# First batch reordered, softmax division moved behind the matrix product, two merged steps per later head pair

## The chip, the cores and the metric

The kernel runs on one core of a Trainium2 chip. Its time is device microseconds of one execution, and the figure of a version is the median of its runs. TensorE (PE) does matrix products and transposes, VectorE (DVE), ScalarE (ACT) and GpSimd (POOL) the elementwise work, and SyncE (SP) issues every DMA. Each engine works through its own list of instructions in order and waits on semaphores for the others.

## The reference

Four batches of 576 tokens with 8 heads of 64 go through three blocks, each fed by the one before:

```python
scores = (q @ k.T) / 8 + alibi          # only 0 <= i-j < 128, else -1e9
attn = exp(scores - max); attn /= (sum + 1e-9); x = attn @ v      # x: B, S, 512
h = gelu(x @ w_in)                      # 1024 wide, halves u and v
v_n = layernorm(v) * g_ln; v_s = w_sg @ v_n + b_sg                # over the tokens
x = x + (u * v_s) @ w_out
xk, xr = token mixes of x with the token before it
out = sigmoid(xr @ w_r) * (relu(xk @ w_k) ** 2 @ w_v)
```

## The kernel before, in words

The program doesn't write the engines' instructions in order. It records operations (`K.mm`, `K.act`, `K.ts`, `K.dma` and so on), each with its engines, an estimated duration and the tiles it touches, and `Rec.schedule` then lays them out on the five engines with a planner. A planned operation starts when its inputs are there by the planner's estimate, and among those ready the one with the lowest due time goes first; `PRI` shifts the due time of all operations of one tile name, `ENG` the choice between engines for operations that two or three engines can do. The result is a fixed order on each engine. On the chip each engine goes through its order and waits where an input is late. SP's order is such a result as well.

Attention works on head pairs: pair `c` is heads 2c and 2c+1, four pairs to a batch, sixteen in all. For a pair, `s_bank` computes scores of query blocks 0 and 1, then of 2 and 3 (tile `s`: two PSUM banks, one per head, with 64-row products running two at a time), and `s_last` those of the last 64 queries of both heads. Each of a pair's nine score tiles goes through `s_tile`: one DVE instruction adds the mask and takes the row maximum, ACT takes the exponential and the row sum. After the ninth, `s_last` takes the reciprocals of the nine sums (`rin`) and multiplies each of the nine tiles `p` by its column of them, on DVE, POOL or ACT. `t1_step`, `t2_step` and `t4_step` transpose the tiles on PE and copy them to SBUF (`pf`); in heads from 8 on the two key blocks of a tile are added first, so there are fewer transposes. `av_step` multiplies by v (tile `a`, 64-column products, two at a time) and copies the result into `x`. `slot(c)` writes the steps of pair c and of pair c-1 into each other: score step, transposes, score step, `av_step`, `s_last`. The score tiles have two PSUM banks (`psS`, tag `s`), which `av_step` uses too, the transposes two (`psT`) and the large products four (`psD`, tag `d`).

In the first batch nothing but attention and the decoding of weights is there to do. Weights come as 64-bit floats for the most part and are decoded by ACT and DVE (`job`; tiles `st`, `wdec`) and split into a high and a low part. So that the granted clock of PE stays high there, `filler` puts in products that nobody reads (tile `wps`). `v_first` begins one product of the second block early: for the first 128 tokens, with the x of head pair 0. Then, for batch b, the steps of the second block (`moe1(b)`) and of the attention of batch b+1 are merged; all products of the second block have the name `d`. The third block (`phase2`, tiles `d`, `rps`, `vps`) comes last.

The lines touched: `PRI`, `ENG` and `NWARM` (L29 to L73), `dma` (L539), `s_bank` and `s_last` (L681 to L715), `av_step` (L767), `slot` (L810), `v_first` and `v_tile` (L860 to L900), and the start of the program from L1072 to L1122.

Of the kernel before, what the change touches and what calls it, by code (L numbers as in the profile page):

```python
# [20 lines left out]
P = 128  # L21
NC = DM // P
HS = S // 2
MW = 320
# [12 lines left out]
    ("rl", "act/dve/pool"): 111000, ("rps", "pe"): 6800, ("s", "pe"): -37200, ("st1", "sp"): 29800, ("sum", "dve"): -135300, ("t", "pe"): -900,
    ("tf", "pe"): -36000, ("tri", "pool"): 3500, ("u", "dve"): -86200, ("v", "dve"): -129400, ("vhl", "act/dve/pool"): -45400, ("vhl", "dve"): -65700,
    ("vhl", "dve/pool"): 5100, ("vps", "pe"): 13200, ("vsg", "dve"): -9100, ("vsg", "dve/pool"): -3900, ("w_in_t", "act/dve/pool"): -1200,
    ("w_in_t", "dve/pool"): -25500, ("w_out_t", "act/dve/pool"): -3600, ("w_out_t", "dve/pool"): 13000, ("w_r_t", "act/dve/pool"): 31700,  # L40
# [6 lines left out]
}  # L47
ENG = {
    ("gg", "act/dve/pool", "act"): -36800, ("gg", "dve/pool", "dve"): -10300, ("k2h", "act/dve/pool", "act"): 63400,
    ("k2h", "act/dve/pool", "dve"): 200, ("k2h", "act/dve/pool", "pool"): 5800, ("k2l", "dve/pool", "dve"): -5500, ("k2l", "dve/pool", "pool"): 1100,  # L50
    ("mask", "dve/pool", "dve"): -13500, ("mask", "dve/pool", "pool"): -157800, ("mask4", "dve/pool", "dve"): 31200,
    ("mask4", "dve/pool", "pool"): -24500, ("mt", "dve/pool", "dve"): -7700, ("mt", "dve/pool", "pool"): 20200, ("p", "dve/pool", "dve"): -400,
    ("p", "dve/pool", "pool"): -14300, ("p", "dve/pool/act", "dve"): 13600, ("p", "dve/pool/act", "pool"): -19400, ("pf", "act/dve", "act"): -9900,
    ("pf", "act/dve", "dve"): 2900, ("pf", "pool/dve", "pool"): 31900, ("pf1", "act/dve", "act"): -143000, ("pf1", "act/dve", "dve"): 1800,
    ("pf4", "act/dve", "dve"): 17100, ("pf4", "pool/dve", "dve"): -54300, ("pf4", "pool/dve", "pool"): -27600, ("rl", "act/dve/pool", "act"): -149000,
    ("rl", "act/dve/pool", "dve"): 13300, ("v", "dve/pool", "dve"): -58600, ("v", "dve/pool", "pool"): 6000, ("vhl", "act/dve/pool", "act"): 10600,
    ("vhl", "act/dve/pool", "dve"): 63200, ("vhl", "act/dve/pool", "pool"): -48100, ("vhl", "dve/pool", "dve"): -52100,
    ("vhl", "dve/pool", "pool"): -500, ("vsg", "dve/pool", "dve"): -5400, ("vsg", "dve/pool", "pool"): 2200, ("w_in_t", "act/dve/pool", "act"): 2400,
    ("w_in_t", "act/dve/pool", "dve"): -21000, ("w_in_t", "dve/pool", "dve"): 18300, ("w_in_t", "dve/pool", "pool"): -98500,
    ("w_out_t", "act/dve/pool", "act"): 5100, ("w_out_t", "act/dve/pool", "dve"): 67600, ("w_out_t", "act/dve/pool", "pool"): -8800,  # L60
    ("w_out_t", "dve/pool", "dve"): -6500, ("w_out_t", "dve/pool", "pool"): -29500, ("w_r_t", "act/dve/pool", "act"): 1800,
    ("w_r_t", "act/dve/pool", "dve"): 2500, ("w_r_t", "act/dve/pool", "pool"): -33900, ("w_r_t", "dve/pool", "dve"): 36800,
    ("w_r_t", "dve/pool", "pool"): 17500, ("w_sg_t", "act/dve/pool", "act"): -19200, ("w_sg_t", "act/dve/pool", "dve"): -5300,
    ("w_sg_t", "act/dve/pool", "pool"): -800, ("w_sg_t", "dve/pool", "dve"): 23300, ("w_sg_t", "dve/pool", "pool"): -12000,
    ("w_v_t", "act/dve/pool", "act"): 54500, ("w_v_t", "act/dve/pool", "dve"): -11700, ("w_v_t", "act/dve/pool", "pool"): -4800,
    ("w_v_t", "dve/pool", "dve"): 18100, ("w_v_t", "dve/pool", "pool"): 10600, ("wk", "act/dve/pool", "act"): -28900,
    ("wk", "act/dve/pool", "dve"): 39900, ("wk", "act/dve/pool", "pool"): 3200, ("wk", "dve/pool", "pool"): 47700, ("x", "act/dve", "act"): 31200,
    ("x", "act/dve", "dve"): -9800, ("xg", "act/dve/pool", "act"): 8000, ("xg", "act/dve/pool", "dve"): -31100, ("xk", "act/dve/pool", "act"): -9400,
    ("xk", "act/dve/pool", "pool"): 25000, ("xk", "dve/pool", "dve"): -11200, ("xk", "dve/pool", "pool"): 5100, ("xr", "act/dve/pool", "act"): -7800,
    ("xr", "act/dve/pool", "dve"): -115500, ("xr", "act/dve/pool", "pool"): 4400, ("xr", "dve/pool", "dve"): -130300,  # L70
    ("xr", "dve/pool", "pool"): 129000,
}
# [1150 lines left out]
```

## Time and profile before

| | us |
|---|---|
| median of 3 runs (lowest, highest) | 606.44 (606.31, 608.42) |
| the profiled execution | 603.6 |
| its span, first to last instruction | 601.9 |
| PE busy in the span | 586.0 |
| DVE, ACT, POOL busy | 407.3, 307.7, 188.0 |

The profile is of one execution. Busy time is the time in which at least one instruction of the engine runs; a share over the whole span is a mean over stages with different limits, so the stages have to be looked at apart. The chain of waits goes back from the last instruction to what released it, step by step. In a timeline a row is a run of like instructions, its start, its length, and in brackets how long the engine stood idle before it and for what. An exact fp32 product shows as two records in the trace, so `s x8` is a score step of four products, and `a x24` an `av_step` of twelve.

### The profile page before, as it was taken

The numbers are of one execution on the slowest core, as the hardware profiler recorded it, in microseconds if no ns is written. First come the engines' busy times: TensorE is split into PE (matmuls) and PEld (weight loads), VectorE is DVE, ScalarE is ACT, GpSimd is POOL, SyncE is SP. The second block draws the span as 40 slices with busy tenths as digits, with TensorE's granted clock in tenths as the row PEclk, the third lists the DMA queues.
The fourth block names the chain that finished last, engine by engine and source line by source line (L and its number), as shares of the span: only waits on it lengthen the run. The fifth ranks groups of instructions, "written<-read, shape, count | busy, mean of one in ns | idle before, by whom it ended". The sixth has DMA issues, their size and how long they took to land.

```text
span 601.9 us, 9953 instructions
## 1 busy us (share of the span) xinstructions
PE 586.0 (97%) x3542; PEld 485.1 (81%) x3542; DVE 407.3 (68%) x1105; ACT 307.7 (51%) x809; POOL 188.0 (31%) x340
## 2 busy tenths in 40 slices
PE   6888999999999999999999999999999999999997
PEld 3555678998789987999889988888888888888885
DVE  4887899885898858887699988980780382243120
ACT  2997888445783446742265457650432451361130
POOL 4352556242641523423032511420450150021010
PEclk8998999999999999999999999999999999999999
DMA  8954433104220231000652265330001100000100
GB/s 223 347 128 118 133 80 97 46 18 140 63 62 2 62 113 50 3 22 1 212 182 71 71 209 182 111 105 36 35 4 67 37 0 36 35 1 0 53 19 35
DMA packets 23281, 48.28 MB, mean 80 GB/s; under 512 B 4416, under 2 KB 13120, under 8 KB 22720
## 3 DMA queue, kind: packets, MB, share of 16 engines
q1 hardware_dynamic: 23232, 47.65, 26.0%
q8 instruction: 28, 0.46, 0.3%
q14 instruction: 21, 0.17, 0.1%
HBM read 38.20 MB, written 9.45 MB: 79 GB/s over the span
## 4 chain that ended last, share of the span: by engine, by line
PE 91%; DMA 3%; DVE 2%; SPq 1%; ACT 1%; issue 1%; POOL 0%; DVEq 0%; POOLq 0%
PE d L431 54%; PE vps L431 17%; PE rps L431 8%; PE s L431 6%; PE a L431 4%; PE tf L439 2%; DMA st<-in_w_in_dram 1%; DMA wraw<-in_w_sgT_dram 1%; SPq L541 1%; DMA rawqk<-in_qk_dram 1%; PE t L439 1%; DVE p L723 0%; POOL w_sg_t L475 0%; PE wps L551 0%; DVE wdec L509 0%
## 5 line engine op out<-in xcount | busy, mean ns | idle before, releaser
L431 PE MATMUL d<-xk,wk 128*128 128x512 f32 (+1 forms) x480 | 103.4, 368 | 0.0
L431 PEld LDWEIGHTS d<-xk,wk 128*128 128x128 f32 x480 | 84.7, 188 | 16.2
L431 PE MATMUL vps<-w_v_t,k2h 128*128 128x512 f32 x288 | 94.8, 396 | 0.0
L453 ACT ACTIVATE p<-p,nmax 128x128 f32<-128x128 f32 (+1 forms) x144 | 67.7, 472 | 22.9 <-DVE nmax L723 21.3
L473 DVE TENSOR_TENSOR r<-vps,r 128x512 f32<-128x512 f32 x18 | 12.3, 690 | 98.3 <-PE vps L431 98.3
L529 POOL TENSOR_SCALAR mt<-xc,mus 128x512 f32<-128x512 f32 (+7 forms) x59 | 45.6, 786 | 63.3 <-DVE k2l L473 36.6
L431 PEld LDWEIGHTS vps<-w_v_t,k2h 128*128 128x128 f32 x288 | 54.1, 188 | 12.7
L431 PE MATMUL d<-w_sg_t,vhl 128*128 128x288 f32 x448 | 63.9, 298 | 0.0
L431 PEld LDWEIGHTS d<-w_sg_t,vhl 128*128 128x128 f32 x448 | 60.4, 188 | 2.4 <-issue 1.6
L431 PE MATMUL d<-w_in_t,xg 128*128 128x512 f32 (+1 forms) x240 | 61.1, 405 | 0.1
L723 DVE CUSTOM_DVE_ANT_0 p<-s,mask 128x256 f32<-128x256 f32 (+1 forms) x144 | 49.9, 378 | 15.9 <-PE s L431 15.7
L453 ACT ACTIVATE rl<-d 128x512 f32<-128x512 f32 (+1 forms) x40 | 22.0, 554 | 72.5 <-PE d L431 67.1
L431 PE MATMUL vps<-w_v_t,k2l 128*128 128x512 f32 x144 | 57.0, 396 | 0.0
L431 PE MATMUL d<-xg,w_in_t 128*128 128x288 f32 x384 | 55.5, 299 | 0.0
L431 PEld LDWEIGHTS d<-xg,w_in_t 128*128 128x128 f32 x384 | 51.8, 188 | 3.9 <-issue 3.2
L431 PE MATMUL d<-gg,w_out_t 128*128 128x288 f32 x384 | 54.7, 297 | 0.0
L431 PE MATMUL s<-rawqk 64*128 64x256 f32 (+2 forms) x320 | 47.2, 388 | 7.5 <-DVE nmax L723 3.9
L431 PEld LDWEIGHTS d<-w_in_t,xg 128*128 128x128 f32 (+1 forms) x240 | 42.0, 180 | 14.9 <-issue 2.5
L431 PEld LDWEIGHTS d<-gg,w_out_t 128*128 128x128 f32 x384 | 51.8, 188 | 2.0 <-issue 1.9
L492 POOL TENSOR_SCALAR_AFFINE_SELECT pf<-pf 128x512 f32<-128x512 f32 (+2 forms) x78 | 41.0, 537 | 34.3 <-ACT pf L461 28.7
L431 PE MATMUL rps<-w_r_t,xr 128*128 128x512 f32 x216 | 50.9, 390 | 0.0
L431 PEld LDWEIGHTS rps<-w_r_t,xr 128*128 128x128 f32 x216 | 40.3, 188 | 8.7 <-ACT r L453 0.2
(116 smaller groups left out, 938.7 us busy)
## 6 DMA issues: line engine op xcount, KB each, us to landing
rawqk<-in_qk_dram SPq DMA_DIRECT2D x32, 288.0 KB, 4.8
rawv<-in_v_dram SPq DMA_DIRECT2D x32, 160.0 KB, 2.3
xs<-x SPq DMA_DIRECT2D x4, 1154.0 KB, 5.5
out_dram<-r SPq DMA_DIRECT2D x18, 256.0 KB, 2.0
st<-in_w_in_dram SPq DMA_DIRECT2D x8, 512.0 KB, 8.6
wraw<-in_w_k_dram SPq DMA_DIRECT2D x8, 512.0 KB, 5.0
wraw<-in_w_v_dram SPq DMA_DIRECT2D x8, 512.0 KB, 3.5
wraw<-in_w_out_dram SPq DMA_DIRECT2D x8, 256.0 KB, 3.1
```

The source lines that it names most:

```text
L431: pe.matmul(real(o), real(l), real(r), start=st, stop=sp, **ex)
L439: pe.transpose(real(o), real(i), real(d))
L453: nc.scalar.activation(real(out), real(in_), func, scale=scale, **kw)
L473: alts.append(("dve", self._dve(out.n, False), lambda: nc.vector.tensor_tensor(real(out), real(a), real(b), op)))
L492: nc.gpsimd.affine_select(out=real(out), in_=real(in_), pattern=[[0, rows], [sgn, n]], compare_op=cmp, fill=0.0, base=0, channel_multiplie ...
L529: alts.append(("pool", 240 + out.n if ptr else 150 + 0.83 * out.n, lambda: nc.gpsimd.tensor_scalar(real(out), real(a), real(s1), real(s2), ...
L541: return self.r.op([("sp", nbytes / 330.0, lambda: nc.sync.dma_start(out=real(out), in_=real(in_)))], [in_, *reads], [out, *writes], nomin ...
L723: K.raw("dve", 70 + w / 0.96, lambda: nc.vector.tensor_tensor_reduce(out=real(pw), in0=real(s), in1=real(ma), scale=-0.125, scalar=3.0e38, ...
```

## The change

Five parts. One: SP's first three DMAs are fixed: the two halves of q and k of pair 0, then `rel`, the table of distances from which the masks are made; all others come behind. Two: for pairs 0 to 3 the tiles `p` of the first 512 queries are no longer multiplied by the reciprocals. `r_rows` spreads the reciprocals over rows by eight small products with the identity (tile `rt`), copies them to SBUF, and the copy of `a` into `x` becomes a multiplication by them on DVE. The tile of the last 64 queries is multiplied as before. Three: `v_first` begins three of the five tiles of the second block's v half for batch 0, with each of the head pairs 0, 1, 2 in turn; the filler goes on until the fifth of these tiles. Four: for pairs from 5 on `slot` has two steps that use 64-wide products in place of four: `av_s` (the product with v of pair c-1 together with the scores of blocks 0 and 1 of pair c) and `s_rest` (the last 64 queries and blocks 2 and 3). Five: all numbers of the planner's tables are new, and the tables tell the first batch (`.0`) and the second block of batch 0 (`.1`) from the rest.

```diff
 PRI = {
-    ("xr", "act/dve/pool"): -2300, ("xr", "dve/pool"): -17600, ("xs0", "sp"): -70700, ("xs1", "sp"): 26500, ("xs2", "sp"): 18000,
...
+    ("xs0.1", "sp"): 49179, ("xs1", "sp"): 2862, ("xs2", "sp"): 8293, ("xs3", "sp"): 14178,
...
-NWARM = 12
+NWARM = 8
+RROW = 4
+MERGE = 5
...
-        return self.r.op([("sp", nbytes / 330.0, lambda: nc.sync.dma_start(out=real(out), in_=real(in_)))],
-                         [in_, *reads], [out, *writes], nominal=nominal)
+        o = self.r.op([("sp", nbytes / 330.0, lambda: nc.sync.dma_start(out=real(out), in_=real(in_)))],
+                      [in_, *reads], [out, *writes], nominal=nominal)
+        if len(self.FIRST) < 3:
+            o.order |= set(self.FIRST[-1:])
+            self.FIRST.append(o)
+        else:
+            o.order.add(self.FIRST[-1])
+        return o
...
-        for n, i, col in [(2 * c + j, i, 4 * j + i) for j in range(2) for i in range(4)] + [(2 * c, 4, 8)]:
+        RS[c] = r
+        for n, i, col in [(2 * c + j, i, 4 * j + i) for j in range(2) for i in range(4) if c >= RROW] + [(2 * c, 4, 8)]:
             pj = PT[n, i]
             K.ts(pj, pj, r[:, col:col + 1], 1.0, ALU.mult, ALU.mult, "dpa")
+    def r_rows(c):
+        t = T("psT", [P, 4, P], F32, "t", "rt")
+        K.mm([(t[64 * j:64 * j + 64, i, :], RS[c][:, 4 * j + i:4 * j + i + 1].spread(64), ident, True, True, SG)
+              for i in range(4) for j in range(2)])
+        rt = T("tp", [P, 512], F32, "t", "rt")
+        K.copy(rt, t.flat())
+        return rt
...
+    def s_rest(c):
+        bank, last = last_items(c, "psT")
+        banks, it = s_items(c, (2, 3))
+        K.mm(last + it)
+        s_tiles(c, (2, 3), banks)
+        rawqk.pop(c)
+        tail_tile(c, bank)
+    def av_s(c):
+        a, a4b, it = av_items(c - 1, "psT")
+        banks, its = s_items(c, (0, 1))
+        AV.append(K.mm(it + its))
+        av_copy(c - 1, a, a4b)
+        s_tiles(c, (0, 1), banks)
...
-        K.copy(x_t[b][:, ch, 1:513], a.flat())
+        if c < RROW:
+            K.tt(x_t[b][:, ch, 1:513], a.flat(), rt, ALU.mult)
+        else:
+            K.copy(x_t[b][:, ch, 1:513], a.flat())
...
+        m = cur and has and c >= MERGE
...
+        if m:
+            trans()
+            add(2800, av_s, c)
+            add(1500, s_rest, c)
+            add(0, tail)
+            return steps
...
-        if n == 3:
-            K.filler_end(wps[:, 0:256], *warm[:2], AV[1])
-            wps = T("psD", [P, 512], F32, "d", "wps")
-            v_first(0, 1)
-            K.filler(wps[:, 0:256], *warm)
+        if n > 1:
+            v_first(range(n - 2, n - 1))
```

What it makes of the order is seen in three places. SP at the start of the program, before (`st` is w_in, `rawqk` q and k of a pair, `rawv` v of a head):

```order
L541 DMA rel<-in_rel_dram 128x320
L541 DMA rawv<-in_v_dram 128x320 x4
L541 DMA ident<-in_ident_dram 128x128
L541 DMA rawqk<-in_qk_dram 64x1152 x2
L541 DMA st_152<-in_w_in_dram 128x1024
L541 DMA rawqk<-in_qk_dram 64x1152 x4
L541 DMA st_152<-in_w_in_dram 128x1024 x3
```

And now:

```order
L581 DMA rawqk_109<-in_qk_dram 64x1152 x2
L581 DMA rel<-in_rel_dram 128x320
L581 DMA st_132<-in_w_in_dram 128x1024 x3
L581 DMA rawqk<-in_qk_dram 64x1152 x2
L581 DMA ident<-in_ident_dram 128x128
```

q and k of pair 0 went from behind six DMAs to the front; three pieces of w_in moved ahead of q and k of pair 1, and the identity and v behind those.

PE behind the first `av_step`, before (`wps` from L551 is filler, `t` transposes, `s` scores):

```order
L431 MATMUL s<-rawqk 64x192 x2
L551 LDWEIGHTS tri
L551 MATMUL wps<-tri 128x256
L431 MATMUL s<-rawqk 128x128 x2
L431 MATMUL s<-rawqk 128x256 x2
L551 LDWEIGHTS tri
L551 MATMUL wps<-tri 128x256
```

The same place now, up to the products of the reciprocals (`rt`) ahead of the second `av_step`:

```order
L469 MATMUL s<-rawqk 64x192 x2
L477 MATMUL t<-ident,p 128x128 x7
L469 MATMUL s<-rawqk 128x128 x2
L469 MATMUL s<-rawqk 128x256 x2
L477 MATMUL t<-ident,p 128x128 x7
L469 MATMUL d<-w_in_t,xg 128x512 x6
L477 MATMUL tf_465<-ident,p 128x128
L469 MATMUL s<-rawqk 128x256 x4
L469 MATMUL d<-w_in_t,xg 128x512 x3
L469 MATMUL rt<-ident,rin 64x128 x8
```

Where filler stood, products `d` of the second block stand now; nine of them are placed ahead of the second `av_step`, 27 ahead of the end of the fourth, where there were none and nine. In all 86 filler and warm-up products have become 41.

PE from the `av_step` of pair 4 on, before (`a_1089` is its last part):

```order
L431 MATMUL a_1089<-pf_1006,rawv 64x64 x4
L431 MATMUL s<-rawqk 64x192 x2
L431 MATMUL d<-w_in_t,xg 128x512 x6
L431 MATMUL s<-rawqk 128x128 x2
L431 MATMUL s<-rawqk 128x256 x2
L431 MATMUL d<-w_in_t,xg 128x512 x6
L431 MATMUL d<-w_in_t,xg 64x512 x6
L439 MATMUL tf<-ident,p 128x128 x4
L431 MATMUL d<-w_in_t,xg 64x512 x6
L439 MATMUL tf<-ident,p 128x128 x4
L431 MATMUL s<-rawqk 128x256 x4
```

And now:

```order
L469 MATMUL a_978<-pf_940,rawv 64x64 x4
L469 MATMUL s<-rawqk 128x128 x2
L469 MATMUL s<-rawqk 128x256 x2
L469 MATMUL d<-w_in_t,xg 128x512 x12
L469 MATMUL s<-rawqk 64x192 x2
L469 MATMUL s<-rawqk 128x256 x4
L469 MATMUL d<-w_in_t,xg 64x512 x12
```

Three stretches of 64-wide products per pair have become two, and both score banks of pair 5, which stood ahead of the `av_step` of pair 4 before (those shown before are pair 6's), stand in and behind it now.

## Rows read from the trace of the kernel before

**Rows 1.** The page: busy time by engine, and the chain that ended last
```profile
PE 586.0 (97%) x3542; PEld 485.1 (81%) x3542; DVE 407.3 (68%) x1105; ACT 307.7 (51%) x809; POOL 188.0 (31%) x340
...
PE 91%; DMA 3%; DVE 2%; SPq 1%; ACT 1%; issue 1%; POOL 0%; DVEq 0%; POOLq 0%
```
**Rows 2.** Stretches: length, busy PE, PEld, DVE, ACT, POOL (instructions); clock, DMA share, GB/s
```profile
0.00:10.70 10.70, 6.73 (x20) 3.08 (x21) 3.25 (x10) 1.28 (x1) 6.02 (x17) 0.92 0.80 218
...
17.80:65.00 47.20, 40.17 (x311) 26.86 (x308) 40.19 (x146) 41.73 (x132) 19.16 (x31) 0.96 0.64 177
75.00:90.00 15.00, 15.00 (x103) 11.18 (x103) 14.66 (x48) 12.59 (x39) 8.30 (x18) 1.00 0.32 80
75.20:134.30 59.10, 59.10 (x453) 51.17 (x455) 53.46 (x168) 39.00 (x124) 27.47 (x53) 1.00 0.23 61
```
**Rows 3.** PE's waits over the whole span: us in total, times, longest
```profile
PE s L431 <- DVE nmax L723: 3.9, 4, 1.4
PE s L431 <- DMA rawqk<-in_qk_dram: 2.7, 1, 2.7
```
**Rows 4.** Groups of PE's instructions between 17.8 and 64.5 us: the filler
```profile
L551 PE MATMUL wps<-tri 128*128 128x256 bf16 x59 | 7.9, 273 | 0.0
```
**Rows 5.** Timeline of the start: start us, length us, what [idle before it]
```profile
3.58 1.19 SPq L541 DMA_DIRECT2D rawqk<-in_qk_dram  x2
...
8.96 2.39 PE L431 MATMUL s<-rawqk 64*128 64x128 f32 x8 [2.66 <-DMA rawqk<-in_qk_dram]
```
**Rows 6.** Timeline of ACT: the ninth exponential of pair 0 and of pair 4
```profile
17.37 0.46 ACT L453 ACTIVATE p<-p,nmax 128x192 f32<-128x192 f32 x1 [0.37 <-DVE nmax L723]
...
64.53 0.46 ACT L453 ACTIVATE p<-p,nmax 128x192 f32<-128x192 f32 x1 [0.28 <-DVE nmax L723]
```
**Rows 7.** Groups of ACT's instructions between 17.8 and 64.5 us
```profile
L536 ACT ACTIVATE p<-p,rin 128x256 f32<-128x256 f32 (+1 forms) x19 | 7.8, 474 | 0.8 <-DVE rin L713 0.8
...
L461 ACT COPY pf<-t 128x384 f32<-128x384 f32 (+1 forms) x11 | 5.4, 513 | 2.0 <-PE t L439 1.9
L625 ACT ACTIVATE wdec<-st 128x512 f32<-128x512 f32 x7 | 4.7, 668 | 0.0
L461 ACT COPY x<-a 128x512 f32<-128x512 f32 (+1 forms) x7 | 2.6, 415 | 0.0
```
**Rows 8.** Groups of DVE's instructions: the page's costliest, then three between 17.8 and 64.5
```profile
L473 DVE TENSOR_TENSOR r<-vps,r 128x512 f32<-128x512 f32 x18 | 12.3, 690 | 98.3 <-PE vps L431 98.3
...
L463 DVE COPY pf<-t 128x512 f32<-128x512 f32 (+1 forms) x5 | 3.2, 662 | 1.7 <-PE t L439 1.6
...
L473 DVE TENSOR_TENSOR p<-p 128x128 f32<-128x128 f32 (+1 forms) x10 | 2.9, 292 | 0.0
...
L526 DVE TENSOR_SCALAR p<-p,rin 128x256 f32<-128x256 f32 (+1 forms) x4 | 1.2, 329 | 0.0
```
**Rows 9.** Timeline of POOL and PE ahead of the av_step of pair 4
```profile
70.39 0.43 POOL L465 TENSOR_SCALAR w_out_t<-wdec 128x256 fp32r<-128x256 f32 x1
...
74.75 0.30 POOL L492 TENSOR_SCALAR_AFFINE_SELECT pf<-pf 128x128 f32<-128x128 f32 x1
...
75.13 1.08 PE L431 MATMUL a<-pf,rawv 128*64 128x256 f32 x8
```
**Rows 10.** Timeline of PE around the 64-wide steps of a later pair
```profile
110.83 3.88 PE L431 MATMUL d<-w_sg_t,vhl 128*128 128x288 f32 x28
...
116.54 0.54 PE L431 MATMUL s<-rawqk 64*64 64x192 f32 x4
117.02 1.32 PE L431 MATMUL d<-w_sg_t,vhl 128*128 128x288 f32 x8
118.27 0.93 PE L431 MATMUL s<-rawqk 64*128 64x128 f32 x8
119.12 1.85 PE L431 MATMUL d<-w_sg_t,vhl 128*128 128x288 f32 x12
...
121.78 1.13 PE L431 MATMUL s<-rawqk 64*128 64x256 f32 x8
```

More of the change, by code (lines that the diff above doesn't have):

```diff
@@ L37 @@
[L37 to L40, printed above, removed]
@@ L51 @@
[L51 to L54, printed above, removed]
@@ L137, in real @@
                 a = a.bitcast(x)
+            elif k == "bro":
+                a = a.to_broadcast([a.shape[0], x])
             elif x == 3:
@@ L192, in op @@
         o.port = {a[0]: self.ports(a[0], reads, writes, single) for a in alts}
-        o.lab = writes[0].base.name if writes and isinstance(writes[0], Vw) else "out"
+        o.lab = (writes[0].base.name if writes and isinstance(writes[0], Vw) else "out") + self.phase
         o.w0 = writes[0].base if writes and isinstance(writes[0], Vw) else None
@@ L690, in s_bank, with last_items, s_tiles @@
                 it.append((banks[j][:, k, :w], rawqk[c][r, 0, q0:q0 + P], rawqk[c][r, 1, k0:k0 + w], True, True, {}))
-        K.mm(it)
+        return banks, it
+    def last_items(c, pool):
+        bank = T(pool, [P, 2, 256], F32, "s" if pool == "psS" else "t", "s")
+        raw = rawqk[c]
+        it = []
+        for j in range(2):
+            r = slice(64 * j, 64 * j + 64)
+            it.append((bank[r, 0, 0:192], raw[r, 0, 512:576], raw[r, 1, 384:576], True, True, SG))
+        return bank, it
+    def s_tiles(c, ii, banks):
         if ii[0] == 0:
@@ L698, in s_bank, with tail_tile @@
                 s_tile(c, 2 * c + j, i, banks[j][:, k, :w], mask[:, h, c0:c0 + w], 4 * j + i)
[L700 to L708 removed]
+    def tail_tile(c, bank):
         s_tile(c, 2 * c, 4, bank[:, 0, 0:192], mask4[:, 2 * c % H // 2, :], 8)
@@ L779, in av_step, with av_copy @@
             a4.append((64 * j, rv, (p4[:, 1, j, :], p4[:, 0, j, :])))
-        a4b = T("psS", [P, 2, 256], F32, "s", "a4")[:, 0, 0:64]
-        AV.append(K.mm([x for y in zip(*its) for x in y] +
-                       [(a4b[r0:r0 + 64], rv[:, 3 + k, :], pf[k], k == 0, k == 1, SG) for k in range(2) for r0, rv, pf in a4]))
+        a4b = T(pool, [P, 2, 256], F32, "s" if pool == "psS" else "t", "a4")[:, 0, 0:64]
+        return a, a4b, ([x for y in zip(*its) for x in y] +
+                        [(a4b[r0:r0 + 64], rv[:, 3 + k, :], pf[k], k == 0, k == 1, SG) for k in range(2) for r0, rv, pf in a4])
+    def av_step(c):
+        a, a4b, it = av_items(c, "psS")
+        rt = r_rows(c) if c < RROW else None
+        AV.append(K.mm(it))
+        av_copy(c, a, a4b, rt)
+    def av_copy(c, a, a4b, rt=None):
+        b, ch = 2 * c // H, c % (H // 2)
         if ch == 0:
@@ L817, in add, with trans @@
             steps.append((w, lambda: f(*a)))
-        if cur:
-            add(1000, s_bank, c, (0, 1))
-        if has:
+        m = cur and has and c >= MERGE
+        def trans():
             for j in range(2):
@@ L824, in slot, with tail @@
             add(120, t4_step, prev)
+        def tail():
+            load_pair(c + 2)
+            load_v(2 * c + 2)
+            load_v(2 * c + 3)
+        if m:
[4 more added lines that the diff above has]
+            return steps
+        if cur:
+            add(1000, s_bank, c, (0, 1))
+        if has:
+            trans()
         if cur:
@@ L856, in v_mms, with v_first @@
         group(ps, [(XG[b][:, kk, pa, s * P:s * P + m], w_in_t[:, kk, pb, DM:DF]) for kk in ks for pa, pb in PASS], 6, ks[0] == 0, ks[-1] == NC - 1)
-    V0 = []
-    def v_first(a, z):
-        if not V0:
-            V0.append(T("psD", [P, 512], F32, "d"))
-        v_mms(V0[0], 0, 0, P, range(a, z))
-        return V0[0]
+    V0 = {}
+    def v_first(ks):
+        for s in range(3):
+            if s not in V0:
+                V0[s] = T("psD", [P, 512], F32, "d")
+            v_mms(V0[s], 0, s, P, ks)
     def moe1(b):
@@ L878, in v_tile @@
             m = min(P, S - s * P)
-            if b == 0 and s == 0:
-                ps = v_first(1, NC)
+            if b == 0 and s in V0:
+                ps = V0[s]
+                v_mms(ps, b, s, P, range(NC - 1, NC))
             else:
@@ L1122, in attn_gmlp_rwkv_kernel @@
     K.filler_end(wps[:, 0:256], *warm[:2], AV[3])
+    wps2 = T("psD", [P, 512], F32, "d", "wps")
+    K.filler(wps2[:, 0:256], *warm)
     for b in range(B):
@@ L1128, in attn_gmlp_rwkv_kernel, with v_last @@
         d = moe1(b)
+        R.phase = ".1" if b == 0 else ""
         if b == 0:
+            def v_last(f):
+                f()
+                K.filler_end(wps2[:, 0:256], *warm[:2], next(o for o in reversed(R.ops) if o.pe))
+            d[4] = (d[4][0], lambda f=d[4][1]: v_last(f))
             for i in range(5):
```

114 lines of the change are left out of this document (70 added, 44 removed), and 26 rows, old and new, of the table PRI.

## The prediction

> **What bounds the kernel now.** First the page: PE is busy 586.0 of 601.9 us, and 91% of the chain that ended last is PE [rows 1]. A change can gain where PE stands idle or does what nobody needs, or by taking work off PE. The view of PE's waits says where the idle time is: scores that wait for DVE to empty their banks, 3.9 us, and the first scores, which wait 2.7 us for q and k [rows 3], all ahead of 70 us; from 75.2 to 134.3 PE is busy for 59.1 of 59.1 us [rows 2]. So from there on every microsecond of PE work costs one, and before that PE isn't the bound. Third the stretches. I mark the first batch by ACT's ninth exponential of a pair: pair 0's ends at 17.8, pair 4's at 65.0 [rows 6]. In these 47.2 us ACT is busy 41.73 (88%), DVE 40.19 (85%), PE 40.17 of which 7.9 are filler [rows 2, 4]. PE does useful work for some 32 us there and fifteen are hollow. Fourth, behind 75 us DVE is close behind PE: 14.66 of 15 us from 75 to 90, 53.46 of 59.1 from 75.2 to 134.3 [rows 2].
>
> The sum below is made against the profiled execution (603.6 us, span 601.9); the median of the runs, 606.44, lies 2.8 above it, and I carry the difference over unchanged. I follow the moment at which the product with v of pair 4 begins, 75.2 in the trace of before [rows 9], since from there to the end PE has no gap in either version if the forecast holds.
>
> **1. q and k first.** Their DMAs are issued at 3.58 and the scores begin at 8.96 [rows 5]; now they are issued first. But that doesn't move pair 0's ninth exponential by as much: ACT's order puts three decodes of w_in ahead of it, and the third needs the third piece of w_in. Ahead of and with that piece SP issues 576 KB of q and k, 160 KB of distances and 3 x 512 KB of w_in, 2.33 MB. At 218 GB/s, the mean of the first 10.7 us [rows 2], that is there at 10.7. Then one decode of 0.67 [rows 7], three exponentials of about 0.5 and one of 0.46 [rows 6] with its sum read: 13.5, and 0.8 for waits on DVE between them: 14.3, against 17.8. Gain 3.5. Ends: 5.8, if the pieces land sooner and only ACT's own work counts, and 0, if the identity and q and k of pair 1, which are issued later than before, hold the transposes up.
>
> A rule of the Trainium skill speaks against it (DMA: Bandwidth & Descriptors, Queues, rings and completion order): a DMA is split over the rings of up to 16 engines, and completion isn't first-in first-out, so the first issued need not be the first complete. The trace has q and k land 5.4 us after their issue with six DMAs ahead of them, which fits a queue in order as well. By the rule, with nothing gained from the place in the queue, term 1 is 0; that is rival C.
>
> **2. The division behind the product.** Per pair eight multiplications of p go; one stays. Of 36 in the four pairs ACT has 19, together 7.8 us [rows 7], DVE 4, 1.2 us [rows 8], POOL the rest. By the order ACT keeps one: -7.4. Also off ACT go four 512-wide copies of `a` (all seven copies take 2.6 [rows 7], the four about 2.3); onto it come three copies of `rt` and four transposed tiles that DVE copied before, seven at 0.51 [rows 7], +3.6. ACT: 41.7 - 6.1 = 35.6. DVE loses 1.2, four of its five tile copies (2.6) and six of ten additions of p (1.8), and gains four multiplications of a PSUM tile (0.69 each by the nearest form, 2.8) and one copy of `rt` (0.7) [rows 8]: 40.2 - 2.1 = 38.1. I take the weight pieces that change engines as even. So DVE, not ACT, sets the least time of this stretch: 39.0 at the 97.7% it reaches from 75 to 90, 44.8 at the 85% that it has here. PE's share rises too: eight `rt` products are 16 records in pairs, 8 x 0.105 (128 columns at half of the 0.21 below) and a change of mode, 1.1 us, four times: 4.4; 18 products `d` are moved in (part 3), 4.3; its 32 become 41 by busy time. Busy time counts each pipelined end, and 4% of the stretch is at the lower clock [rows 2], so some 37 of real work. Three engines over 80% that wait for each other don't reach 97.7%. I take 43.0, a little under DVE's 85%: -4.2. Ends: -8.2, and 0 if in-order waits and not loads set the pace. What hides the 4.4 us of `rt` is the hollow; if that is gone, they count in full.
>
> The wait that this adds: the multiplication into `x` waits for `rt`, so for the ninth tile's sum. Behind it in DVE's order stand the high-low split of x and the score tiles of the next pair; the 0.5 us copy is planned ahead of `a`, which ends 2 us later, so I cost it at nothing.
>
> **3. Three v tiles early.** Between pair 4's ninth exponential and its product with v lie 10.2 us now (65.0 to 75.2), ended by a triangle cut on POOL at 74.75 [rows 9]. PE spends them on products `d`, two thirds of which are done before that now. So the chain through POOL is what is late next. Ahead of the cuts POOL has six other things from 70.39 on (first row of [rows 9]; lengths 0.43, 0.74, 0.46, 0.19, 0.59, 0.28, in all 2.7); in the new order scales and cuts follow each other directly there. 10.2 - 2.7 = 7.5. Gain 2.7; ends 0 (the chain unchanged) and 4.3 (the 18 products). The pair-4 product begins at 14.3 + 43.0 + 7.5 = 64.8, 10.4 earlier than 75.2.
>
> The count of `d` ahead of it is 36 in both orders, but pair 5's two score steps, 0.85 and 1.06 long by their starts, now come behind it: +1.9.
>
> **4. Merged steps.** A run of 28 `d` takes 3.82 to the next row's start, 0.136 each [rows 10]. From 117.02 to 119.12 there are 8 of them, 1.09, and a score step. Steps of 768 and 1024 columns last 0.85 and 1.06, so 256 columns take 0.21 and 768 take 0.63: 0.37 is lost, and a little in the first `d` behind, 0.4 for entering and leaving the 64-wide form. Per pair one such stretch goes. But inside the merged ones the form changes as well: the last-queries step takes 0.48 for 2 x 192 columns, 0.32, so 0.15 for a change inside; there are two per pair where there was one. 0.4 - 0.15 = 0.25, eleven pairs (5 to 15): -2.8. Ends: 0 and -4.4.
>
> The Trainium skill has the rule that any change of the tiling mode, not only of the tile, drains the array (TensorEngine Tiling (Array Packing), Key Properties). The trace agrees for the change inside a stretch (0.15). Taken as one price for each change, 0.2, a pair has 7 changes before and 6 now, and the term is -2.2, the result 0.6 later.
>
> **5. DVE behind 75 us.** From the product of pair 4 to that of pair 7 PE has 59.1 us now; 36 products of 0.136 fewer stand there and three merges: 53.4. DVE's work there I leave at 53.46, at its best share of 97.7%: 54.7. So PE waits 1.3. Ends 0, and 5.7 at the 90.5% that it has now.
>
> Fewer filler products (86 to 41) cost nothing while useful products stand in their place.
>
> **Sum:** -10.4 + 1.9 - 2.8 + 1.3 = -10.0. Profiled 593.6, median 596.4.
>
> **The rivals.**
> A: DVE runs as full in the first batch as behind it, 39.0 in place of 43.0: 592.4. For it: POOL has far less to do there. Against: nothing in the stretch is over 88% now.
> B: the stretch doesn't shrink, since each pair waits in turn for its scores, transposes and banks: +4.2, 600.6. For it: PE's waits for DVE to empty the score banks [rows 3], and the same banks now. Against: the nine scales stood in that chain, and are gone from it.
> C: the place in the queue gives nothing (above): +3.5, 599.9. By the same trace the first DMA's data was not the last to come.
> D: DVE holds PE behind 75 us with the share it has now: +4.4, 600.8. With B: 605.0, no change.
> E, the other side: the merged steps stall. In each of eleven `av_s` the scores of pair c stand behind the product with v of pair c-1, which needs the last cut on POOL; in the trace that cut ends at 75.05 and the product begins at 75.13 [rows 9], so nothing is to spare there. If PE waits 1.5 us at each, and the next softmax starts late by as much, 16.5 come back: 612.9. It decides from 0.9 us per pair. Against: PE has no wait behind 75 us, and there is other work for 7 us between the steps to put ahead.
> Also on that side, small: with filler gone the granted clock may fall to 1.2 GHz; 0.96 in the stretch now means 4 us of it [rows 2].
>
> **Chances.** Forecast (594 to 599) 0.50; A 0.18; B 0.11; C 0.06; D 0.06; B with D or the clock, no change, 0.04; E 0.05. About 0.5% or 3 us is what can be told from no change. Faster: 0.50 + 0.18 + 0.11 + 0.06 + 0.06 = 0.91, less 0.02 for the edges of B to D: 0.89. Same 0.06, slower 0.05. The range reaches from A with the early ends of 1 and 4 (589) to B with half of D (602.8, say 603). The forecast's own is 592 to 600.
>
> **What would show it.** In the new profile: first scores near 5 us and pair 0's ninth exponential near 14.3 (term 1); pair 4's near 57, ACT's L574 scales down to four or so ahead of that, DVE over 85% (term 2); the product with v of pair 4 near 65, with the cut on POOL ending just ahead (term 3); score stretches twice per pair (term 4); PE's waits between 65 and 115 about 1.3 us and DVE near 97% there (term 5). PE waits in `a` or `s` behind 120 us would make the prediction wrong, and so would pair 4's exponential later than 60 us.

## The result and the profile after

The changed kernel takes 601.65 us (median of 4 runs, 600.97 to 602.57), the kernel before 606.38 beside it: a ratio of 0.9916, 95% interval 0.9889 to 0.9943, or 4.7 us faster. That is the side that was forecast and about half of its size (10.0). The profiled execution took 602.57, its span is 600.8.

The page after: busy time, DMA's busy tenths in 40 slices of 15 us, and the chain.

```profile
PE 581.8 (97%) x3561; PEld 484.2 (81%) x3561; DVE 413.0 (69%) x1105; ACT 307.7 (51%) x800; POOL 184.4 (31%) x321
...
DMA  8974523222122130000652155150002000000100
...
PE 87%; DMA 6%; DVE 2%; POOL 1%; ACT 1%; SPq 1%; issue 0%; DVEq 0%; ACTq 0%
```

PE is 4.2 us less busy than in [rows 1] (filler and warm-up 6.1 less, `rt` 4.4 more, the rest in the clock and in overlaps), and DMA's share of the chain has doubled from 3% to 6%. PE's waits over the span (us in total, times, longest), against [rows 3]:

```profile
PE t L477 <- ACT pf L499: 2.9, 1, 2.9
PE a L469 <- POOL pf L530: 2.3, 3, 1.4
PE s L469 <- DMA rawqk<-in_qk_dram: 2.0, 3, 1.1
...
PE s L469 <- DVE nmax L813: 1.2, 1, 1.2
...
PE rps L469 <- ACT r L491: 1.2, 1, 1.2
...
PE a L469 <- POOL mv L1009: 0.7, 1, 0.7
...
PE d L469 <- DVE v L547: 0.5, 1, 0.5
```

The score banks are waited for 1.2 us in place of 3.9. New are 2.9 us for one copy of transposed tiles, and waits behind 75 us, where there were none. The stages, by the marks of the prediction (columns as in [rows 2]): the first batch from pair 0's ninth exponential to pair 4's, then to pair 4's product with v, to pair 5's, and to pair 7's.

```profile
14.97:62.51 47.54, 41.09 (x333) 28.71 (x333) 36.77 (x131) 34.89 (x115) 11.26 (x24) 0.93 0.74 188
62.51:67.78 5.27, 4.29 (x27) 3.27 (x26) 4.52 (x14) 4.23 (x12) 2.86 (x7) 1.00 0.93 229
67.78:86.15 18.37, 16.96 (x114) 12.56 (x114) 17.02 (x56) 13.04 (x39) 14.69 (x28) 1.00 0.29 80
86.15:124.39 38.24, 38.05 (x303) 33.98 (x303) 33.95 (x109) 26.99 (x88) 21.52 (x37) 1.00 0.27 76
```

ACT and DVE had as much work taken off as was reckoned (34.9 and 36.8 us busy, 35.6 and 38.1 forecast), and yet the stretch lasts 47.5 us, where it lasted 47.2 [rows 2]. So the load of neither sets it. What does is in the timelines (start, length, what, idle before it). First a row of SP in the kernel before, then SP, ACT, DVE, POOL and PE in the changed one:

```profile
18.12 1.06 SPq L541 DMA_DIRECT2D wraw<-in_w_sgT_dram  x2
```

```profile
18.19 0.47 SPq L581 DMA_DIRECT2D rawqk<-in_qk_dram  x1
24.35 0.80 SPq L581 DMA_DIRECT2D rawv<-in_v_dram  x2
25.20 1.75 SPq L581 DMA_DIRECT2D rawqk<-in_qk_dram  x3
27.16 4.44 SPq L581 DMA_DIRECT2D wraw<-in_w_sgT_dram  x2
...
37.99 0.43 ACT L499 CAST w_sg_t<-wraw 128x288 fp32r<-128x288 f32 x1 [2.92 <-DMA wraw<-in_w_sgT_dram]
...
38.46 0.78 DVE L511 TENSOR_TENSOR w_sg_t<-wraw,w_sg_t 128x288 fp32r<-128x288 f32 x1 [2.34 <-ACT w_sg_t L499]
...
37.61 0.43 POOL L503 TENSOR_SCALAR w_sg_t<-wraw 128x288 fp32r<-128x288 f32 x1 [6.04 <-DMA wraw<-in_w_sgT_dram]
...
39.63 1.11 PE L477 MATMUL t<-ident,p 128*128 128x128 f32 x4 [2.91 <-ACT pf L499]
```

Three engines stand still together for the first pieces of `w_sg`. In the new order SP issues these behind two loads of v; their buffers come free with pair 0's product, so SP stands from 18.7 to 24.35 and `w_sg` is issued at 27.16; its first piece is taken up at 37.6, 10 us later. It used to be issued at 18.12, ahead of the loads of v. Behind ACT's waiting instruction stand the copies of transposed tiles, and PE waits for those; from 39.7 to 43 the granted clock is then 0.5, that is 1.2 GHz.

### The profile page after: what moved, and what is told of

It reads as the page before. It is cut to its first block, busy times and chain, and to the rows that moved or that the text cites. A ratio compares the mean times of both kernels' runs of the same rounds, so it can differ in the third digit from the quotient of the medians.

```text
span 600.8 us, 9962 instructions
## 1 busy us (share of the span) xinstructions
PE 581.8 (97%) x3561; PEld 484.2 (81%) x3561; DVE 413.0 (69%) x1105; ACT 307.7 (51%) x800; POOL 184.4 (31%) x321
## 4 chain that ended last, share of the span: by engine, by line
PE 87%; DMA 6%; DVE 2%; POOL 1%; ACT 1%; SPq 1%; issue 0%; DVEq 0%; ACTq 0%
PE d L469 50%; PE vps L469 17%; PE rps L469 8%; PE s L469 5%; PE a L469 5%; DMA st<-in_w_in_dram 2%; DMA rawqk<-in_qk_dram 2%; PE tf L477 2%; DMA wraw<-in_w_sgT_dram 1%; SPq L581 1%; DMA rawv<-in_v_dram 1%; POOL pf L530 1%; PE t L477 1%; PE rt L469 0%; DVE gt L547 0%
## 5 line engine op out<-in xcount | busy, mean ns | idle before, releaser
L469 PE MATMUL d<-xk,wk 128*128 128x512 f32 (+1 forms) x480 | 101.6, 368 | 0.0
L491 ACT ACTIVATE p<-p,nmax 128x256 f32<-128x256 f32 (+1 forms) x144 | 67.7, 473 | 22.6 <-DVE nmax L813 22.2
L567 POOL TENSOR_SCALAR mt<-xc,mus 128x64 f32<-128x64 f32 (+7 forms) x48 | 34.8, 732 | 95.3 <-DVE k2l L511 55.4
L813 DVE CUSTOM_DVE_ANT_0 p<-s,mask 128x256 f32<-128x256 f32 (+1 forms) x144 | 48.0, 381 | 14.5 <-PE s L469 14.3
L469 PE MATMUL rps<-w_r_t,xr 128*128 128x512 f32 x216 | 54.9, 393 | 1.2 <-ACT r L491 1.2
L469 PE MATMUL d<-xg,w_in_t 128*128 128x288 f32 x384 | 54.7, 298 | 0.5 <-DVE v L547 0.5
L469 PE MATMUL s<-rawqk 64*128 64x256 f32 (+2 forms) x320 | 44.5, 385 | 3.2 <-DMA rawqk<-in_qk_dram 2.0
L511 DVE TENSOR_TENSOR k2l<-rl,k2h 128x512 fp32r<-128x512 f32 (+1 forms) x40 | 24.9, 636 | 32.2 <-ACT k2h L499 31.9
```

Source lines behind the costliest of these rows:

```text
L469: pe.matmul(real(o), real(l), real(r), start=st, stop=sp, **ex)
L491: nc.scalar.activation(real(out), real(in_), func, scale=scale, **kw)
L511: alts.append(("dve", self._dve(out.n, False), lambda: nc.vector.tensor_tensor(real(out), real(a), real(b), op)))
L567: alts.append(("pool", 240 + out.n if ptr else 150 + 0.83 * out.n, lambda: nc.gpsimd.tensor_scalar(real(out), real(a), real(s1), real(s2), ...
L813: K.raw("dve", 70 + w / 0.96, lambda: nc.vector.tensor_tensor_reduce(out=real(pw), in0=real(s), in1=real(ma), scale=-0.125, scalar=3.0e38, ...
```

## The experiments

Most experiments change the finished order and nothing else: a few instructions are moved in the lists, all the rest stays. The marks of each traced execution (us; "to the end" is the span less the start of pair 4's product; ratio to the kernel before, run beside it):

| | 9th exp, pair 0 | product of pair 1 | of pair 2 | of pair 4 | to the end | median (runs) | ratio, 95% interval |
|---|---|---|---|---|---|---|---|
| before | 17.8 | 35.7 | 48.2 | 75.1 | 526.8 | 606.4 (4) | |
| r1, before again | 17.4 | 36.7 | 49.2 | 76.0 | 526.6 | 605.2 (12) | 0.9997 (0.998 to 1.002) |
| after | 15.0 | 32.8 | 47.6 | 67.8 | 533.0 | 601.7 (4) | 0.9916 (0.989 to 0.994) |
| r2, after again | 16.2 | 32.1 | 47.7 | 67.5 | 532.9 | 601.4 (12) | 0.9920 (0.989 to 0.995) |
| r3, w_sg earlier | 17.4 | 35.5 | 45.7 | 66.1 | 533.1 | 599.0 (6) | 0.9900 (0.986 to 0.994) |
| r4, steps split | 14.3 | 30.1 | 43.8 | 64.0 | 537.3 | 603.2 (12) | 0.9977 (0.995 to 1.001) |
| r5, w_sg and two waits | 15.9 | 35.6 | 45.8 | 66.2 | 531.4 | 598.8 (6) | 0.9857 (0.982 to 0.990) |
| r6, q, k place undone | 19.2 | 34.8 | 45.7 | 66.2 | 533.0 | 601.0 (4) | 0.9913 (0.989 to 0.994) |
| r7, before, q, k first | 16.9 | 38.6 | 51.1 | 77.6 | 527.1 | 607.0 (10) | 1.0016 (0.999 to 1.004) |
| r8, v tiles late | 15.8 | 29.8 | 44.3 | 68.3 | 533.1 | 603.1 (1) | |
| r9, half of w_in out | 15.5 | 33.2 | 43.5 | 63.8 | 533.2 | 597.4 (5) | 0.9855 (0.983 to 0.988) |
| r10, before, the same | 19.3 | 38.6 | 51.1 | 77.6 | 526.8 | 606.2 (10) | 1.0003 (0.999 to 1.002) |
| r11, no reciprocal rows | 16.2 | 32.2 | 47.2 | 66.3 | 533.0 | 600.3 (6) | 0.9902 (0.988 to 0.993) |
| r12, scores earlier | 17.1 | 33.0 | 43.3 | 68.1 | 532.1 | 600.9 (4) | 0.9882 (0.984 to 0.993) |

**The two kernels again.**

> The kernel before, unchanged, once more with a trace. Its profiled execution took 603.6 us and its timed ones 606.0 to 608.4. If executions differ in the first batch (DMA landing times): a span near 604 or 605 with the product with v of pair 4 starting 2 to 3 us later than 75.2 and the same distance from there to the end (526.7). If the 603.6 was the odd one among executions that differ all over: the end moves without pair 4's product.

> The changed kernel, unchanged, once more with a trace. Ratio to before 0.989 to 0.994. In the first trace ACT, DVE and POOL stood still together from 35 to 38 us for the first pieces of w_sg. If that wait belongs to the order of the DMAs it is there again, 2.5 us or more on ACT; if it was an accident of one execution it is gone and the span is some 3 us shorter.

Both come out near their first form: r1's product of pair 4 is later by 0.9, not 2 to 3, and the distance from there is the same. From pair 4's product to the end a kernel takes the same in every trace, 526.6 to 527.1 and 532.9 to 533.2 with all edits that lie ahead of it; the traced executions differ only up to there. ACT's wait for `w_sg` is there again in r2, 2.47 us ahead of 36.83. So the change gains 7.3 to 8.6 us up to pair 4's product and gives 6.2 back behind it.

**The place of q and k.** In r6 three kinds of DMA go back ahead of q and k of pair 0; in r7 q and k go first in the kernel before.

```diff
+    move(lambda sp: lab(sp, "rel") + lab(sp, "rawv")[:4] + lab(sp, "ident"), lambda sp: sp[0])   # r6
...
+    move(lambda sp: lab(sp, "rawqk")[:2], lambda sp: sp[0])                                       # r7
```

> The changed kernel with only SP's first places changed back: the distances, the four loads of v and the identity go ahead of q and k of pair 0, as they stood before. Theory (a queue that is worked off nearly in order): 0.7 MB more ahead of q, k and the three pieces of w_in, 3 us at 218 GB/s; first scores at 8 in place of 5 to 6, the ninth exponential of pair 0 at 17 to 18 in place of 15.0, the product of pair 0 by 2 to 3 later, and the time 2 to 3 longer. Rival (the place in the queue gives nothing, since DMAs share all rings): first scores and ninth exponential within 1 us of where they are, time unchanged. Third: the loads of v and the identity, which come sooner, give back what q and k lose, so that the first scores are later and the product of pair 0 is not.

> The kernel before with one edit: the two halves of q and k of pair 0 are SP's first two DMAs. Nothing else is moved. First scores near 5.5 in place of 8.5 to 9. If the first scores set the start (term 1 of the forecast in its simplest form): product of pair 0 and the end 2.5 to 3.5 earlier, 602. If something behind them does (the pieces of w_in that ACT decodes ahead of the exponentials, q and k of pair 1): product of pair 0 within 1 us, time within 1 us.

The marks move as the queue's order says: pair 0's ninth exponential to 19.2 in r6, and r7's first scores to 5.83 from 8.5 to 9. The time doesn't: 601.0 against 601.4 to 601.7, and 607.0 against 606.5 beside it. In r6 pair 2's product is even sooner than in the changed kernel. A start that is 3 us earlier runs into something that doesn't depend on it. Nor is the place of `w_sg` behind the loads of v enough for the wait: in r6 it is kept, the issue is 3 us later, and ACT finds the piece there, since POOL has the first one 5.6 us after its issue and not 10.

```profile
30.11 1.05 SPq L581 DMA_DIRECT2D wraw<-in_w_sgT_dram  x2
...
36.94 0.41 ACT L499 CAST w_sg_t<-wraw 128x288 fp32r<-128x288 f32 x1
```

From 25 to 30 us the DMA share is 0.64 in r6, and 1.08 in the changed kernel. In r7, as in r10 below, pair 2's product comes 1.9 to 2.9 us later than in the two traces of the kernel before; the medians don't show it, and no run says why.

**What the first batch waits for.** r3 moves two DMAs; r5 moves two more instructions; r12 adds one step on PE.

```diff
+    move(lambda sp: lab(sp, "wraw")[:2], lambda sp: lab(sp, "st1")[2])         # r3, r5, r12: w_sg ahead of w_in's last two
...
+        order.insert(last + 1, o)       # r5, r12, POOL: one mv behind the cuts of pair 5
+        del order[at]
...
+    order.remove(pe[rest])
+    order.insert(at, pe[rest])          # r12, PE: last scores of pair 5 ahead of six d
...
+    order.remove(r)
+    order.insert(to, r)                 # r5, r12, ACT: the first sigmoid ahead of three for relu squared
```

> The changed kernel with only two DMAs moved on SP: the first two pieces of w_sg go ahead of the last two pieces of w_in, and so ahead of the loads of v that wait for pair 0's product. All other engines keep their order. Theory (a load behind a waiting load): ACT's 3.7 us of idleness at 34 to 38 goes, the product of pair 2 starts near 44.5 in place of 47.6, and the time falls by 2.5 to 3.5 us, to about 598.5. Rival (the DMA engines are at 96% there, so what comes earlier makes other pieces late): the last pieces of w_in are now waited for, pair 2's product starts within 1 us of 47.6, no change of time. Second rival (the gain is lost before pair 5 to the cuts on POOL): pair 2's product early by 3, pair 5's product not, time within 1 us.

> The changed kernel with the two pieces of w_sg earlier, as in the run before, and two more moves. On POOL one small product of the layer norm, 0.94 us in the trace, goes from between the cuts of pair 5 to behind them. On ACT the first sigmoid of the third block, with its load of a table, goes ahead of three instructions for relu squared, because PE waits 1.2 us for it at 372. If these waits cost what PE stands there: product of pair 5 starts 0.9 closer to that of pair 4 (18.4 now, 17.5), PE's 1.2 us at 372 gone, and 2 us less than with the w_sg move alone, about 597. If the chain only moves its waiting (PE then waits at the next product for the relu tiles, or for the layer norm): within 0.5 us of it.

> The run with w_sg and two waits moved, with one more edit on PE: the step with the last scores of pair 5 goes ahead of six of the twelve products d that stand between it and the first scores of pair 5. PE waits there for cuts of pair 5 on POOL, 1.2 to 1.6 us. If the late scores are what makes these cuts late: the product of pair 5 starts 1 us or more sooner after that of pair 4 (18.2 in the run without this edit), and PE's wait for the cuts falls by as much. If the scores then wait for their banks, which DVE empties: PE waits some 1 us at them and the distance stays within 0.5 us of 18.2.

In r3 ACT's wait is gone and pair 1's product to pair 2's takes 10.2 us in place of 14.8; the start of that execution was slow, so pair 2's product is only 1.9 sooner. The median is some 2.5 lower, which the intervals of the ratios don't separate. In r5 pair 2's product comes at the same 45.8, though pair 0's came 4.3 us sooner than in r3 (20.95 against 25.21): now ACT waits 1.04 us for a piece of w_in at 24.33 and 2.53 for transposes at 30.40. In r12 pair 2 comes at 43.3, and ACT waits 2.69 us for the next pieces of `w_sg`; pair 3's product, 59.1, is later than in any other trace of the changed order:

```profile
44.07 0.43 ACT L499 CAST w_sg_t<-wraw 128x288 fp32r<-128x288 f32 x1 [2.69 <-DMA wraw<-in_w_sgT_dram]
```

So what is moved ahead is paid by what stands behind it, as the rival said, though not to the full. Of the two waits of r5 PE's wait for the sigmoid, at 372, was worth its 1.2 us (533.0 to 531.4 in the table, with the cuts); on POOL pair 5's product came 0.2 sooner and not 0.9. r12's step gave nothing either: 18.6 us from pair 4's product to pair 5's, against 18.15 in r5. Its chain of waits (start, length, what) says why:

```profile
73.16 1.54 PE s L469 x12
74.69 1.61 PE d L469 x6
...
76.32 0.61 ACT gt L491
...
76.95 0.69 DVE gt L547
77.64 0.33 DVE p L813
```

The scores are done at 74.7, but DVE has a piece of the gelu ahead of most of them in its order, and that now waits for the `d` that were moved back. Of the versions that compute all of it r5 has the lowest ratio to the kernel before.

**The transfers.** In r9 and r10 four of w_in's eight pieces bring 32 KB each in place of 512 KB.

```diff
+        return lambda: nc.sync.dma_start(out=real(st1[:, kk].flat()[:, 0:64]), in_=real(src[:, 0:64]))
...
+    zero.eng = ("dve", 0, lambda: nc.vector.memset(real(st1.flat()), 0))
```

> The changed kernel without most of the transfer of four of w_in's eight pieces: each brings 32 KB in place of 512 KB, and the rest of the buffer is set to zero by DVE at 1 to 6 us, where DVE waits for the distances. So 1.9 MB are left out, and part of w_in is zero; all else, and the order on every engine, is as it was. Theory (transfers set the pace of the first half of the first batch, whatever their order): the wait for the first pieces of w_sg is gone, the product of pair 2 starts 3 to 5 us earlier than 47.6, at 43 to 44.5, and the time falls by 3 to 5 us, to 596.5 to 598.5. Rival (the engines' in-order waits set it): product of pair 2 not before 45.7, where the runs with w_sg earlier and with q and k in their old place have it, and the time no lower than theirs (599.0 and 601.0).

> The same 1.9 MB left out of the kernel before. If transfers set its pace too: product of pair 2 at 45 or earlier in place of 48.2 and 49.2, time 3 us lower or more. If ACT and DVE do, which were busy 88% and 85% of the stretch: product of pair 2 within 1 us, time within 1 us.

Here the two kernels part. The changed one gains 3.9 us (0.9855 against 0.9920, intervals apart), the kernel before nothing. With half of w_in out of the way the stretch from pair 0's ninth exponential to pair 4's is 15.46 to 58.52, 43.1 us. ACT in r9:

```profile
15.02 0.44 ACT L491 ACTIVATE p<-p,nmax 128x192 f32<-128x192 f32 x1
...
58.07 0.45 ACT L491 ACTIVATE p<-p,nmax 128x192 f32<-128x192 f32 x1
```

Stretches of 5 us (columns as above; the last two are DMA's share and GB/s), the changed kernel:

```profile
15.00:20.00 5.00, 4.39 (x24) 3.55 (x24) 3.96 (x16) 2.43 (x8) 0.68 (x1) 0.66 1.07 394
20.00:25.00 5.00, 5.00 (x58) 3.56 (x56) 2.72 (x11) 5.00 (x15) 0.58 (x2) 1.00 1.02 203
25.00:30.00 5.00, 4.22 (x31) 2.97 (x29) 5.00 (x19) 4.76 (x19) 2.09 (x4) 1.00 1.08 268
30.00:35.00 5.00, 5.00 (x55) 3.56 (x55) 4.50 (x15) 3.81 (x16) 0.69 (x2) 1.00 1.01 212
35.00:40.00 5.00, 1.70 (x13) 1.10 (x10) 2.51 (x6) 2.08 (x6) 1.23 (x2) 0.96 0.73 152
```

r9, and the kernel before:

```profile
20.00:25.00 5.00, 5.00 (x59) 3.60 (x56) 2.74 (x12) 5.00 (x18) 0.59 (x2) 1.00 0.41 91
...
35.00:40.00 5.00, 4.61 (x37) 3.21 (x34) 4.87 (x16) 4.79 (x13) 0.69 (x2) 1.00 0.59 159
```

```profile
25.00:30.00 5.00, 3.16 (x35) 1.84 (x31) 4.82 (x12) 4.88 (x16) 1.89 (x3) 1.00 1.03 363
30.00:35.00 5.00, 4.16 (x33) 3.30 (x34) 4.40 (x18) 4.96 (x15) 5.00 (x7) 1.00 0.54 87
```

The DMA engines are full to 30 us in the kernel before and to 35 in the changed one. In the first ACT and DVE are nearly full from 25 to 30 as well (4.88 and 4.82 of 5), which fits that less to transfer changes nothing. In the second they are as full there, but from 35 to 40 every engine falls to 1 to 2.5 us of 5, while what they wait for is still on its way; in r9 PE, DVE and ACT are at 4.6 to 4.9.

**The reciprocal rows and the early v tiles.** r11 leaves out the `rt` products and their copies; the multiplication is a plain copy. r8 moves the 27 early products `d` on PE.

```diff
+    order = [o for o in order if o not in LEFT]                     # r11
...
+    early = [o for o in order if o.lab == "d.0"]                    # r8
...
+    at = next(k for k, o in enumerate(order) if o.lab == "d.1")
+    order[at:at] = early
```

> The changed kernel without the reciprocal rows: the eight products for each of four pairs, which take PE 1.09 us per pair in the trace, and the copies of their tile to SBUF, 0.6 us each on ACT or DVE, are left out, and the multiplication into x is a plain copy; so the output is not divided in the first batch. Order of all else kept. Theory (they lie in PE's hollow while transfers set the pace): the time within 1 us, product of pair 4 within 1.5 us. Rival (PE's chain of transposes, scores and products is what sets the pace): 3 to 4.4 us less at the product of pair 4, and 3 us or more at the end.

> The changed kernel with the 27 products of the three early v tiles moved on PE from between the scores of pairs 2 to 4 to just ahead of the products that finish these tiles (62 us in the trace). They take 27 x 0.232 = 6.3 us. If they filled idle time in the first batch: products of pairs 2 and 3 start where they do now, that of pair 4 some 5 to 6 us later, and the end by as much, less what PE idles there now (filler 1.15, waits 1.7): 3 to 5 us. If they stood in the way of the transposes in the first batch: products of pairs 2 and 3 start 1 to 2 us earlier, and the end is less than 2 us later.

Without the rows the median is 1.1 lower than r2's and pair 4's product 1.2 to 1.5 sooner: of PE's 4.4 us for them two thirds to three quarters are hidden, where the forecast had all of them, and the intervals of the two ratios overlap. r8 is one execution; in it the products of pairs 1 to 3 come 2.3 to 4 us sooner than in the changed kernel's two, and pair 4's 0.5 to 0.8 later. Its start was 0.8 to 1.7 sooner. So the early products don't lie in the hollow free of charge: of the 4.4 us that they save between the products of pairs 3 and 4 (9.3 against 13.7), some 2.3 to 3.2 go ahead of that. That they hold transposes up there is the expectation's reading; it isn't shown, and one run leaves the rest open.

**The merged steps.** r4 puts six `d` between the product with v and the scores in each of the eleven.

```diff
+        SPLIT.append((AV[-1], it, its))
...
+        op.eng = (*op.eng[:2], lambda it=it: emit(it), *op.eng[3:])
...
+        order.insert(nx + 1, half)     # half emits its, behind the next six d
```

> The changed kernel with each of the eleven merged steps of the product with v and the scores cut in two: six products d stand between them, so there are three stretches of 64-wide products per pair again, as before the change. The work is the same. The forecast's price of 0.25 us a pair: 2.8 us slower. The price that the rows of the changed kernel suggest (a gap of 0.12 to 0.15 where a stretch is entered): 1.3 to 1.7 us slower. If neither entering nor leaving costs PE anything that isn't covered: within 0.5 us.

To the end r4 takes 537.3 in place of 533.0, and the ratio is 0.0057 higher (3.4 us), with intervals that just touch. Of the 4.3 to the end 1.4 are longer or new waits behind pair 4 (`u` on DVE 1.1, `mv` 0.3). The rest is 2.9, or 0.26 a pair. PE in the changed kernel and then in r4, around pair 7's product:

```profile
124.39 1.97 PE L469 MATMUL a<-pf,rawv 128*64 128x256 f32 x24
126.28 0.93 PE L469 MATMUL s<-rawqk 64*128 64x128 f32 x8
127.14 2.65 PE L469 MATMUL d<-gg,w_out_t 128*128 128x288 f32 x18
```

```profile
121.31 1.97 PE L1272 MATMUL a<-pf,rawv 128*64 128x256 f32 x24
123.20 1.06 PE L469 MATMUL d<-gg,w_out_t 128*128 128x288 f32 x6
124.19 0.93 PE L1272 MATMUL s<-rawqk 64*128 64x128 f32 x8
```

The scores last 0.86 right behind `a` (126.28 to 127.14) and 0.85 alone [rows 10], so nothing is saved inside. What a stretch of its own costs is ahead of it: six `d` take 0.82 at 0.136 each and here 0.99, so 0.17. The 1.0 us between eleven times that and 2.9 isn't assigned.

## Why the prediction was half right

The sign, and the place of the first gain, were right; the measured 601.65 lies in the range and 1.7 above the forecast's own. That it lies in the range is in part luck: it is where B and D were put, and term 3 gained 2.2 more than forecast and hides part of what term 2 missed. Both signs that were to make the prediction wrong are there: pair 4's ninth exponential ends later than 60, at 62.5 and 62.2, and PE waits in `a` behind 120 us, 0.7 ahead of pair 9's product. Term by term:

- **1, q and k first (-3.5).** As a mark right: pair 0's ninth exponential at 15.0 and 16.2, 14.3 forecast. As a term of the sum wrong: r6 and r7 show it worth nothing. That is the outcome of rival C, but not by its mechanism. What was issued first came first (first scores at 4.98 and 5.83), so nothing here shows the rule that the Trainium skill states (DMA: Bandwidth & Descriptors, Queues, rings and completion order).
- **2, the first batch (-4.2).** This is the step that failed. I derived the time from the loads of DVE, ACT and PE; the transfers enter no term, though [rows 2] had their share, a mean of 0.64. By slices of 5 us it is 1.0 to 35 us in the changed kernel, and the first pieces of `w_sg`, issued behind loads that wait, come 10 us after their issue. The stretch came out at 47.5 and 46.0 (r2: 16.17 to 62.17), the outcome of rival B, again by another cause than score banks. What I reckoned for the engines was near: relieved of half of w_in, r9 shows 43.1 where I wrote 43.0. The closeness is luck, since the length depends on the start too: r6, with all transfers and a start 3 us later, has 41.8 (19.19 to 60.94). The granted clock, the small risk beside E, doesn't track the length: the mean over the stretch is 0.93 in both traces of the changed kernel and 0.96 and 0.93 in those of the kernel before, but r11, with 0.89, has 44.8 us, and r3, with 0.94, has 43.5.
- **3, pair 4 (-2.7).** 62.51 to 67.78 is 5.3, not 7.5. Two thirds of the products were out of the way, as said, and the cuts follow each other directly. PE still has nothing useful for part of it: nine filler products (1.15) and 0.68 of waiting for POOL.
- **Together** pair 4's product came at 67.8 and 67.5, not 64.8. In r9 it is at 63.8.
- **4, merged steps (-2.8).** The mechanism, a price for each stretch, was right; its parts were not: where I had 0.4 for entering and leaving less 0.15 for a change inside, the rows show 0.17 ahead of a stretch and nothing inside. That makes 1.9 for eleven pairs; by r4's time it is 0.26 each, 2.9, the forecast's own size. The reading by the Trainium skill's rule (TensorEngine Tiling (Array Packing), Key Properties), one price for each change of mode, gave 2.2; the runs don't choose between that and mine, since merging saves one change of mode by either.
- **5, behind pair 4 (+1.3, and +1.9 for pair 5's scores).** Forecast from there to the end was +0.4 in all; it is +6.2, always. Where PE stood: 1.6 us ahead of pair 5's product, 0.7 ahead of pair 9's, 0.5 at 242 and 1.2 at 373. The first is DVE's, as I had it, with POOL as its last link. The chain of waits (start, length, what) and PE:

```profile
75.81 0.41 DVE p L813
76.22 0.60 DVE gt L547
...
80.72 0.55 DVE bn L1006
81.28 0.97 DVE p L564 x5
82.44 0.46 DVE v L564
82.90 0.61 DVE pf L501
83.58 0.52 POOL pf L530
84.10 0.94 POOL mv L1010
85.03 1.91 POOL pf L530 x4
```

```profile
86.15 0.65 PE L469 MATMUL a<-pf,rawv 128*64 128x256 f32 x2 [1.41 <-POOL pf L530]
86.99 1.96 PE L469 MATMUL a<-pf,rawv 128*64 128x256 f32 x22 [0.19 <-POOL pf L530]
```

From 75.81 on DVE works off pair 5's softmax between the layer norm's pieces, one behind the other; it is busy for 17.02 of 18.37 us between the two products. With DVE that full, it fits that r12's earlier scores and r5's move on POOL gave little. From pair 4's product to pair 7's I forecast 54.7; it is 56.6, of which DVE is busy for 50.97, 90% and not 97.7%. The place is that of rival E (the merged step needs the last cut), at pair 5 and for 0.7 at pair 9 instead of at all eleven. The waits behind it come with the new order, which I didn't follow behind 135 us (r5 shows this for the wait at 372, the other two are argued): I had read that PE has no gap there before and let that stand for after. Waits 4.0, pair 5's scores and what else is left to do behind pair 4 about 1.8 (each product counted at the mean distance of its kind), less 1.9 for the merged steps: 3.9 of the 6.2 (2.9 of it with r4's 2.9 for the steps). The other 2.3 (3.3) lie in spots of 0.1 to 0.3 us, such as pair 4's product itself, 2.53 us long in place of 1.90; I can't assign them one by one.

The sum against the runs: 7.3 to 8.6 us gained up to pair 4's product, 6.2 lost behind it. The traces themselves lie 1.0 apart (603.6 and 602.57) and 2.1 (604.28 and 602.15), less than the medians, by the spread of the start. r2's twelve runs reach from 595.9 to 607.5; only one of them is traced, so where the others differ isn't shown.

## What to carry to other kernels

When work is taken off the engines that bind a stretch, look next at what was not an engine: the transfers by slices of a few us, not the mean of the stretch, and for each load what stands ahead of it in its queue and waits. A start moved forward is worth only what the next thing that doesn't depend on it allows; the test is to undo that part alone. And a new order has to be read to its end: three waits behind 160 us, where there was none, took 2.3 us, about as much as the merged steps gave (1.9 to 2.9).
